# One row of decays a head for pairs 1 to 5 of a decay-attention kernel, the other blocks' masked rows written by GpSimd, and the order of instructions set anew

## The chip, the cores and the metric

The kernel runs on one core of one Trainium2 chip. A core has five engines, each with its own queue of instructions worked off in order: PE (TensorE, matmuls and transposes into PSUM), DVE (VectorE), ACT (ScalarE), POOL (GpSimd) and SP (SyncE, which here only issues DMAs). They meet at semaphores alone. The metric is the device time of one execution in microseconds (us); less is better. Line numbers L... are those of the kernel before, unless said otherwise.

## The reference

Causal attention with a decay for 8 batches of 8 heads, 576 positions, 64 columns a head, and behind it a gated layer with a convolution of 5 taps. Cut to what matters:

```
scores = q @ k.T / sqrt(64)
cum    = cumsum(log(clip(f, 1e-4, 1)))
scores = where(causal, -1e9, scores + cum[:, None] - cum[None, :])
attn   = softmax(scores)                       # per row
x      = attn @ v                              # heads side by side: (8, 576, 512)
gate   = sigmoid(causal_conv5(x, conv_w))
out    = (gate * (x @ w_val)) @ w_out          # float32
```

A constant that is the same in a whole row of scores falls out of the softmax. So a row of the decay needs only -cum of the columns and any reference that is common to the row.

## The kernel before

The work goes by pairs of heads, 32 pairs (4 a batch). The 576 rows of a head's scores are cut in four blocks of 128 rows and a last piece of 64; block j needs its first 128(j+1) columns, so the blocks of a head have 128, 256, 384 and 512 columns (EXT), at columns 0, 128, 384 and 768 of a row of 1280 (BOFF). The last pieces of the two heads of a pair share one tile of 576 columns.

For a pair the steps are these. `load_pair` and `load_rest` load q, k, v and the decays. `plan_t` transposes q and k on PE (L524, L531) and evicts them (Xf for pairs 0 to 3; Xh and Xl, a value and its remainder, from pair 4 on). `plan_s` makes the scores on PE in three groups: blocks 3 and 1 of both heads, blocks 2 and 0, the last pieces. For each block DVE adds the decays to the scores and takes the row's extreme in one instruction (L598, "the reduction"), ACT takes the exponential (L602) into P, and any of POOL, DVE and ACT normalizes P (L376 and L374). `plan_pt` transposes P on PE (L643) and evicts it (L369), `plan_pv` multiplies with v (PV), evicts to x, splits x into xh and xl (L712) and does the convolution's taps (L724 and L376). `plan_moe` runs behind every fourth pair: Mv (x times w_val), h (L769), its split into hh and hl (L782), Mo (h times w_out), and the store. The weights w_val and w_out are loaded and split during the first pairs by DVE, ACT and POOL (L822 to L862).

The decays: a table `decd` of 64 rows, one a head, is written to DRAM at the start. A row has the 1280 columns of the four blocks, each with the block's own reference, and 576 for the last piece. From pair 1 on a head's row is spread over 128 partitions by one DMA into the tile `dm` (640 KB, three buffers dm0 to dm2, taken in turn by heads); a second load fills `dl`. Then POOL masks the diagonal squares of the four blocks in place with two `affine_select` instructions (L428), and adds a triangle to `dl` (L431). Pair 0 has its decays put in by PE, and its `dm1` is a memset to zero (L457) with the same mask.

```python
load("dec", 1.6, p + 0.05 * h, dm[m], decd[2 * i + h:2 * i + h + 1, 0:SW].to_broadcast([P, SW]), dk, [("dm", m)])
pool("sel", 0.8, p + 0.2 + 0.05 * h, sel, [("dm", m)], [("dm", m)])
dkey = [("dm", a)] if u < 2 else [("dl", r, 0), ("dl", r, 1)]
```

What sets the order: the steps are entered into a `Plan` with their durations, priorities and the engines that may do them. `Plan.order` lists them engine by engine on a modelled clock. Tables set it: OFF shifts a step's priority by its class and phase of the program, PEN adds to a step's start time on an engine that it may also run on, STICK favours PE instructions of the mode just run. Each engine then runs its list in order, and a wait holds all that is listed behind it on that engine. Where a step may go to several engines the plan also chooses the engine. DMAs stand in SP's list (some early ones in ACT's).

Of the kernel before, what the change touches and what calls it, by code (L numbers as in the profile page):

```python
# [42 lines left out]
OFF = {  # L43
# [11 lines left out]
    "load": (12.4, 68.46, 92.08, 57.68, 91.65, 143.0), "norm": (-52.85, -16.37, 2.57, -148.6, -15.27, -20.52),  # L55
    "rec": (0.68, 86.96, -11.16, -5.51, -2.16, -38.89), "red": (-0.44, -76.99, -63.6, -16.05, -44.87, 4.92),
    "sel": (37.59, 20.57, -11.72, 7.64, 56.84, 101.1), "sig": (0.0, 0.0, 127.6, 262.5, 85.39, 148.2),
    "st0": (-100.8, 0.0, 0.0, 0.0, 0.0, 0.0), "start": (1.05, 0.0, 0.0, 0.0, 0.0, 0.0),
    "tabD": (-71.18, 0.0, 0.0, 0.0, 0.0, 0.0), "warm": (-150.4, 0.0, 0.0, 0.0, 0.0, 0.0),
# [3 lines left out]
}  # L63
PEN = {
# [4 lines left out]
    ("X", "DVE"): (10.66, 6.42, 35.96, 35.67, 3.07, 32.37), ("conv", "ACT"): (37.06, 9.53, 0.39, 7.85, 12.52, 8.12),  # L69
    ("conv", "DVE"): (0.01, 0.0, 0.02, 0.0, 0.09, 1.39), ("conv", "POOL"): (51.47, 31.7, 58.49, 34.72, 29.95, 35.69),  # L70
    ("hh", "ACT"): (0.0, 0.0, 0.0, 0.0, 0.5, 3.04), ("hh", "DVE"): (0.0, 0.0, 1.73, 16.52, 3.91, 0.39),
    ("hl", "DVE"): (0.0, 0.0, 0.45, 0.87, 4.98, 0.0), ("hl", "POOL"): (0.0, 0.0, 0.0, 0.67, 0.0, 30.02),
    ("load", "ACT"): (1.58, 0.0, 0.0, 0.0, 0.0, 0.0), ("norm", "ACT"): (0.44, 0.25, 1.01, 0.21, 1.1, 2.13),
    ("norm", "DVE"): (6.2, 19.99, 21.87, 2.29, 2.56, 0.18), ("norm", "POOL"): (0.63, 17.37, 0.04, 25.85, 0.46, 2.15),
    ("sel", "DVE"): (36.1, 36.18, 41.87, 17.73, 90.83, 1.24), ("sel", "POOL"): (0.65, 0.76, 0.61, 0.6, 1.44, 6.22),
    ("start", "ACT"): (10.22, 0.0, 0.0, 0.0, 0.0, 0.0), ("start", "DVE"): (4.31, 0.0, 0.0, 0.0, 0.0, 0.0),
    ("start", "POOL"): (5.56, 0.0, 0.0, 0.0, 0.0, 0.0), ("wo", "ACT"): (0.0, 0.0, 5.81, 0.0, 0.0, 0.0),
# [4 lines left out]
}  # L82
# [191 lines left out]
def tile_decay_attention_gated_mlp(  # L274
# [134 lines left out]
    def load_rest(i):  # L409
# [12 lines left out]
        for h in range(2 if i else 1):  # L422
            m = (2 * i + h) % NH if i else 1

            def sel(m=m):
                for lo, n, c in ((0, 256, 0), (256, 512, 384)):
                    t = dm[m][:, lo:lo + 2 * n].rearrange("p (b c) -> p b c", b=2)[:, :, c:c + P]
                    nc.gpsimd.affine_select(out=t, in_=t, pattern=[[0, 2], [-1, P]], base=0, channel_multiplier=1,  # L428
                                            compare_op=ALU.is_ge, fill=-BIG)
            pool("sel", 0.8, p + 0.2 + 0.05 * h, sel, [("dm", m)], [("dm", m)])  # L430
        any_("sel", {"POOL": 0.3, "DVE": 0.14}, p + 0.3, lambda eng: eng.tensor_tensor(  # L431
# [18 lines left out]
    def mk_pick():  # L450
        nc.gpsimd.memset(pick, 0.0)
        for row, cols in ((0, slice(0, P + D)), (D + 1, slice(0, P)), (D + 1, slice(P + D, 2 * P))):
            n = cols.stop - cols.start
            nc.gpsimd.affine_select(out=pick[:, cols], in_=pick[:, cols], pattern=[[0, n]], base=-row, channel_multiplier=1,
                                    compare_op=ALU.not_equal, fill=1.0)
    pool("start", 1.5, z + 0.25, mk_pick, (), [("dm", 0)])
    any_("start", {"POOL": 1.4, "DVE": 0.75}, z + 0.25, lambda eng: eng.memset(dm[1], 0.0), (), [("dm", 1)])  # L457
    any_("start", {"POOL": 0.65, "DVE": 0.4}, z + 0.25, lambda eng: eng.memset(dl[0], 0.0), (), [("dl", 0, 0), ("dl", 0, 1)])
# [459 lines left out]
```

## Time and profile before

| | |
|---|---|
| time, median of 3 runs | 593.08 us (592.48 to 595.91) |
| the profiled execution's own time | 592.27 us |
| its span, first to last instruction | 590.5 us |
| mean granted PE clock | 0.977 |
| loads of `dm`, 640 KB each | 62, 5.4 us from issue to landing (median) |
| POOL selects on `dm` | 126, 481 ns (mean) |

The profile is of one execution. Busy time of an engine leaves out waits and the issuing of DMAs. PEclk is the share of its full clock that PE was granted, in tenths. "Idle before" in a row is the time that the engine stood ahead of these instructions, with what ended it. In a timeline the first two columns are the start and the length of a group in us, and a bracket gives the wait ahead of it.

### The profile page before, as it was taken

Reading aid. Unit: us, or ns where it says so; the run is one execution under the profiler, and the core shown is the slowest. Engines: PE = TensorE matmul, PEld = TensorE weight load, DVE = VectorE, ACT = ScalarE, POOL = GpSimd, SP = SyncE. Lnnn points to the kernel's source line nnn. Section 1 sums busy time; section 2 is a strip of 40 time slices with the busy share of each in tenths; the row PEclk is TensorE's granted clock in tenths of the full one; section 3 lists DMA queues with packets and bytes.
Section 4 is the critical chain, followed back from the end, with each engine's and each line's share of the span. In section 5 each row is a group of like instructions: output and inputs, shape, how many; then the busy total and the mean of one; then the engine's idle time right before and its main releaser. Section 6 shows DMA issues by size and latency. Waiting matters only on the chain.

```text
span 590.5 us, 14025 instructions
## 1 busy us (share of the span) xinstructions
PE 558.2 (95%) x4693; PEld 487.5 (83%) x4693; DVE 461.3 (78%) x1238; ACT 447.9 (76%) x1217; POOL 249.9 (42%) x398
## 2 busy tenths in 40 slices
PE   8778898799889999999999999999999999999997
PEld 7546587689779998889989988899888987889885
DVE  6488979899988797788967897668879789587660
ACT  4688878999878887888887988677798876764511
POOL 3431367334322556456553746455556461210200
PEclk9779699899999999999999999999999999999999
DMA  6979898676465585757866675466776544220012
GB/s 147 266 185 266 170 240 230 166 196 168 114 183 135 143 234 158 188 136 188 188 157 167 184 189 154 117 179 152 193 201 188 159 120 123 80 83 19 37 37 89
DMA packets 136294, 93.43 MB, mean 158 GB/s; under 512 B 118474, under 2 KB 118494, under 8 KB 136222
## 3 DMA queue, kind: packets, MB, share of 16 engines
q1 hardware_dynamic: 136142, 92.52, 59.0%
q8 instruction: 37, 0.61, 0.4%
q14 instruction: 35, 0.29, 0.2%
q10 hardware_dynamic: 80, 0.02, 0.0%
HBM read 82.60 MB, written 9.91 MB: 157 GB/s over the span
## 4 chain that ended last, share of the span: by engine, by line
PE 69%; DVE 13%; DMA 8%; ACT 5%; issue 3%; SPq 1%; POOL 1%; DVEq 0%; POOLq 0%; ACTq 0%
PE banks L354 54%; PE banks L643 9%; DVE banks L598 6%; PE banks L524 3%; DMA wu<-in_moe_w_val_dram 3%; ACT P L602 3%; DMA dm<-decd 2%; DVE gate L724 2%; PE banks L661 2%; DMA qn<-in_q_dram 1%; DVE negm L598 1%; SPq L381 1%; DMA kn<-in_k_dram 1%; PE banks L531 1%; ACT P L374 1%
## 5 line engine op out<-in xcount | busy, mean ns | idle before, releaser
L602 ACT ACTIVATE P<-banks,negm 128x256 f32<-128x256 f32 (+3 forms) x256 | 131.9, 531 | 35.9 <-DVE negm L598 35.6
L369 ACT COPY pt<-banks 128x256 f32<-128x256 f32 (+2 forms) x320 | 116.9, 436 | 42.8 <-PE banks L643 36.4
L598 DVE CUSTOM_DVE_ANT_0 banks<-banks,dm 128x256 f32<-128x256 f32 (+3 forms) x256 | 120.4, 515 | 33.4 <-PE banks L354 22.2
L724 DVE SCALAR_TENSOR_TENSOR gate<-x,cw,gate 128x576 f32<-128x576 f32 x128 | 111.6, 876 | 1.7
L354 PE MATMUL banks<-xh,wall 128*128 128x288 f32 x512 | 110.2, 300 | 1.0 <-ACT ot L369 0.7
L428 POOL TENSOR_SCALAR_AFFINE_SELECT dm<-dm 128x256 f32<-128x256 f32 x126 | 57.5, 481 | 122.0 <-DMA dm<-decd 100.1
L376 POOL TENSOR_SCALAR P<-P,rz 128x128 f32<-128x128 f32 (+3 forms) x132 | 79.0, 614 | 56.5 <-DVE rz L612 32.7
L643 PE MATMUL banks<-ident,P 128*128 128x128 f32 x640 | 93.2, 283 | 9.3 <-POOL P L376 4.1
L354 PE MATMUL banks<-pt,vt 128*64 128x128 f32 (+2 forms) x1408 | 99.0, 294 | 3.2 <-DVE Xl L515 1.9
L354 PEld LDWEIGHTS banks<-pt,vt 128*64 128x64 f32 x1408 | 87.1, 139 | 16.0 <-issue 3.1
L354 PE MATMUL banks<-wall,hh 128*128 128x512 f32 x288 | 92.8, 403 | 2.8 <-ACT P L602 2.6
L643 PEld LDWEIGHTS banks<-ident,P 128*128 128x128 f32 x640 | 74.4, 144 | 20.0 <-POOL P L376 5.3
L354 PEld LDWEIGHTS banks<-xh,wall 128*128 128x128 f32 x512 | 83.8, 188 | 2.8 <-ACT ot L369 1.1
L354 PE MATMUL banks<-xl,wall 128*128 128x288 f32 x256 | 75.4, 294 | 0.0
L712 POOL TENSOR_TENSOR xl<-x,xh 128x576 fp32r<-128x576 f32 x32 | 47.1, 1475 | 46.1 <-ACT xh L369 46.1
L354 PEld LDWEIGHTS banks<-wall,hh 128*128 128x128 f32 x288 | 51.0, 188 | 13.3 <-ACT P L602 3.6
L354 PE MATMUL banks<-Xh 128*128 128x288 f32 (+2 forms) x280 | 59.1, 346 | 1.2 <-DVE Xl L515 1.0
L782 POOL TENSOR_TENSOR hl<-h,hh 128x576 fp32r<-128x576 f32 (+2 forms) x36 | 36.9, 1032 | 48.4 <-ACT hh L369 48.4
L354 PE MATMUL banks<-wall,hl 128*128 128x512 f32 x144 | 56.5, 392 | 0.0
L354 PE MATMUL banks<-Xh,Xl 128*128 128x288 f32 (+2 forms) x280 | 53.6, 315 | 0.0
L354 PE MATMUL banks<-Xl,Xh 128*128 128x288 f32 (+2 forms) x280 | 53.3, 314 | 0.0
L602 ACT ACTIVATION_READ_ACCUMULATOR P<-banks,negm 128x1 f32 x256 | 52.9, 206 | 0.0
(105 smaller groups left out, 916.7 us busy)
## 6 DMA issues: line engine op xcount, KB each, us to landing
dm<-decd SPq DMA_DIRECT2D x62, 640.0 KB, 5.4
out_dram<-ot SPq DMA_DIRECT2D x36, 256.0 KB, 2.1
dl<-decd SPq DMA_DIRECT2D x62, 144.0 KB, 3.8
qn<-in_q_dram SPq DMA_DIRECT2D x64, 128.0 KB, 3.6
kn<-in_k_dram SPq DMA_DIRECT2D x64, 128.0 KB, 5.8
vt<-in_v_dram SPq DMA_DIRECT2D x64, 128.0 KB, 2.9
zn<-in_k_dram SPq DMA_DIRECT2D x32, 32.0 KB, 3.1
vt<-in_v_dram SPq DMA_DIRECT2D x32, 32.0 KB, 3.2
```

Of the source, the lines that this page charges most:

```text
L354: nc.tensor.matmul(out, lhsT=lhsT, rhs=rhs, start=start, stop=stop)
L369: (eng.copy if eng is nc.scalar else eng.tensor_copy)(out=out, in_=in_)
L376: eng.tensor_scalar(out=out, in0=in_, scalar1=col, scalar2=0.0, op0=ALU.mult, op1=ALU.add)
L428: nc.gpsimd.affine_select(out=t, in_=t, pattern=[[0, 2], [-1, P]], base=0, channel_multiplier=1, compare_op=ALU.is_ge, fill=-BIG)
L524: nc.tensor.transpose(out=bank(key)[:, n * P:(n + 1) * P], in_=src[:, n].rearrange("p h d -> p (h d)"), identity=ident)
L598: nc.vector.tensor_tensor_reduce(out=sl, in0=sl, in1=add[:, o:o + ext], op0=ALU.add, op1=ALU.min, scale=-0.125, scalar=3.0e38, accum_out=n ...
L602: nc.scalar.activation(out=dst[:, o:o + ext], in_=bank(key)[:, c0:c0 + ext], func=AF.Exp, bias=negm[r][:, col], scale=-1.0, accum_out=zs[r ...
L643: nc.tensor.transpose(out=bank(key)[:, c:c + P], in_=Pt[m][:, BOFF[b] + P * j:BOFF[b] + P * j + P], identity=ident)
L661: nc.tensor.transpose(out=bank(key)[:, P * j:P * j + P], in_=Pl[r][:, D + P * j:D + P * j + P], identity=ident)
L712: any_("xl", {"POOL": 1.4, "DVE": 0.67}, p, lambda eng: eng.tensor_tensor(out=xl[s], in0=xv, in1=xh[s][:, :].bitcast(F32), op=ALU.subtract ...
L724: eng.scalar_tensor_tensor(out=gt, in0=src, scalar=wt_, in1=gt, op0=ALU.mult, op1=ALU.add)
L782: eng.tensor_tensor(out=hl[jj][:, y:y + x1 - x0], in0=h32[:, x0:x1], in1=hh[jj][:, y:y + x1 - x0].bitcast(F32), op=ALU.subtract)
```

## The change

For pairs 1 to 5 (i < NE = 6) the load of a head's decays brings the row of block 3 alone, 512 columns in place of 1280 (256 KB in place of 640). POOL then writes the masked rows of the blocks 1, 2 and 0 from the first 256, 384 and 128 columns of that row, one `affine_select` each that masks as it copies, and masks the last 128 columns of block 3 in place. The rows of the blocks 0 to 2 thus have block 3's reference. The work stands in two steps of two instructions: blocks 1 and 3, which the first group of reductions needs, and blocks 2 and 0 with a key of their own (`dmb`), which the second group waits for. From pair 6 on everything is as before. The tables OFF and PEN and STICK have other numbers, so every engine's list is another.

```diff
+NE = 6
-STICK = 18.18
+STICK = 20.75
 OFF = {
-    "H": (0.0, 0.0, 6.66, 25.1, 5.83, 28.91), "Mo": (0.0, 0.0, 0.53, 3.6, 3.84, 5.39),
+    "H": (0.0, 0.0, -20.85, -33.12, -47.53, -65.58), "Mo": (0.0, 0.0, -16.69, 18.48, 3.88, 41.67),
...
-            load("dec", 1.6, p + 0.05 * h, dm[m], decd[2 * i + h:2 * i + h + 1, 0:SW].to_broadcast([P, SW]), dk, [("dm", m)])
+            lo = BOFF[3] if i < NE else 0
+            load("dec", 1.6 * (SW - lo) / SW, p + 0.05 * h, dm[m][:, lo:], decd[2 * i + h:2 * i + h + 1, lo:SW].to_broadcast([P, SW - lo]), dk,
+                 [("dm", m), ("dmb", m)])
...
-            pool("sel", 0.8, p + 0.2 + 0.05 * h, sel, [("dm", m)], [("dm", m)])
+
+            def spread(blocks, m=m):
+                for j in blocks:
+                    t = dm[m][:, BOFF[3]:BOFF[3] + EXT[j]]
+                    if j == 3:
+                        t = t[:, L0 - P:]
+                        nc.gpsimd.affine_select(out=t, in_=t, pattern=[[-1, P]], base=0, channel_multiplier=1,
+                                                compare_op=ALU.is_ge, fill=-BIG)
+                    else:
+                        nc.gpsimd.affine_select(out=dm[m][:, BOFF[j]:BOFF[j] + EXT[j]], in_=t, pattern=[[-1, EXT[j]]], base=P * j,
+                                                channel_multiplier=1, compare_op=ALU.is_ge, fill=-BIG)
+            if 0 < i < NE:
+                pool("sel", 0.75, p + 0.2 + 0.05 * h, lambda spread=spread: spread((1, 3)), [("dm", m)], [("dm", m)])
+                pool("sel", 0.9, p + 0.25 + 0.05 * h, lambda spread=spread: spread((2, 0)), [("dm", m)], [("dmb", m)])
+                continue
+            pool("sel", 0.8, p + 0.2 + 0.05 * h, sel, [("dm", m)], [("dm", m), ("dmb", m)])
...
-                dkey = [("dm", a)] if u < 2 else [("dl", r, 0), ("dl", r, 1)]
+                dkey = [("dm", a), ("dmb", a)][:1 + u] if u < 2 else [("dl", r, 0), ("dl", r, 1)]
```

In all, 10 of the 62 loads of `dm` are of 512 columns; POOL has 106 of the old selects, not 126, and 40 new ones (10 of 256, 10 of 384 and 20 of 128 columns). The counts of steps that moved from one engine to another are small: eight more first taps of the convolution on ACT and eight fewer on DVE, four more full `hh` casts on DVE and four fewer on ACT, the memset of `dm1` on POOL and not on DVE.

SP's list ahead of and behind the load of `dm2`, the decays of pair 1's first head (vt1 is pair 1's v, dl1 its last pieces' decays, ot the first piece of w_val). Before:

```order
L381 DMA kn1_76<-in_k_dram 128x4x64 x2
L381 DMA zn1_78<-in_k_dram 64x2x64
L381 DMA vt1_92<-in_v_dram 128x4x64
L381 DMA dm2_70<-decd_67 128x1280
L381 DMA dl1_72<-decd_67 64x576 x2
L381 DMA vt1_92<-in_v_dram 128x4x64
L381 DMA vt1_92<-in_v_dram 64x2x64
L381 DMA ot_125<-in_moe_w_val_dram 128x1024
L381 DMA dm0_68<-decd_67 128x1280
L381 DMA dm1_69<-decd_67 128x1280
```

And now:

```order
L385 DMA kn1_76<-in_k_dram 128x4x64 x2
L385 DMA zn1_78<-in_k_dram 64x2x64
L385 DMA vt1_92<-in_v_dram 128x4x64 x2
L385 DMA dm2_70<-decd_67 128x512
L385 DMA dl1_72<-decd_67 64x576 x2
L385 DMA vt1_92<-in_v_dram 64x2x64
L385 DMA ot_125<-in_moe_w_val_dram 128x1024
L385 DMA dm0_68<-decd_67 128x512
L385 DMA dm1_69<-decd_67 128x512
```

Both halves of pair 1's v stand ahead of the load of `dm2`, not one; the three loads of decays are the shorter ones.

POOL's list at the same place. P0 and P1 are pair 0's P, Pl0 its last pieces, rz0 its row sums' reciprocals; dm2 and dm0 are pair 1's decays, dm1 the first head's of pair 2. Before:

```order
L376 TENSOR_SCALAR P0_83<-P0_83,rz0_97 128x512
L428 AFFINE_SELECT dm2_70<-dm2_70 128x2x128 x2
L376 TENSOR_SCALAR P0_83<-P0_83,rz0_97 128x256
L376 TENSOR_SCALAR P1_84<-P1_84,rz0_97 128x256
L376 TENSOR_SCALAR P0_83<-P0_83,rz0_97 128x128
L376 TENSOR_SCALAR P1_84<-P1_84,rz0_97 128x384
L376 TENSOR_SCALAR P1_84<-P1_84,rz0_97 128x128
L376 TENSOR_SCALAR Pl0_86<-Pl0_86,rz0_97 128x576
L428 AFFINE_SELECT dm0_68<-dm0_68 128x2x128 x2
L428 AFFINE_SELECT dm1_69<-dm1_69 128x2x128 x2
```

And now (L442 masks block 3, L445 writes another block):

```order
L380 TENSOR_SCALAR P0_83<-P0_83,rz0_97 128x512
L445 AFFINE_SELECT dm2_70<-dm2_70 128x256
L442 AFFINE_SELECT dm2_70<-dm2_70 128x128
L445 AFFINE_SELECT dm2_70<-dm2_70 128x384
L445 AFFINE_SELECT dm2_70<-dm2_70 128x128
L380 TENSOR_SCALAR P1_84<-P1_84,rz0_97 128x256
L380 TENSOR_SCALAR P0_83<-P0_83,rz0_97 128x128
L380 TENSOR_SCALAR P1_84<-P1_84,rz0_97 128x128
L380 TENSOR_SCALAR Pl0_86<-Pl0_86,rz0_97 128x576
L445 AFFINE_SELECT dm0_68<-dm0_68 128x256
L442 AFFINE_SELECT dm0_68<-dm0_68 128x128
L445 AFFINE_SELECT dm1_69<-dm1_69 128x256
```

Two of pair 0's normalizations left POOL (ACT has them), and the selects on `dm2` are four. Further on the second two selects of a head may stand behind the first two of the next head: for `dm0` here, and likewise for `dm2` of pair 2, whose rows are now:

```order
L883 TENSOR_TENSOR wall_126<-gate1_114,ot_125 128x512
L445 AFFINE_SELECT dm2_70<-dm2_70 128x256
L442 AFFINE_SELECT dm2_70<-dm2_70 128x128
L445 AFFINE_SELECT dm0_68<-dm0_68 128x256
L442 AFFINE_SELECT dm0_68<-dm0_68 128x128
L445 AFFINE_SELECT dm2_70<-dm2_70 128x384
L445 AFFINE_SELECT dm2_70<-dm2_70 128x128
L445 AFFINE_SELECT dm0_68<-dm0_68 128x384
```

Here `dm0` is the first head of pair 3, and the blocks 2 and 0 of `dm2` come behind its first select.

DVE's list in pair 7, where the first batch's gated layer begins (h32 is the product with the gate, dm0 and dm2 pair 7's decays). Before:

```order
L769 TENSOR_TENSOR h32_116<-banks_129,gate0_113 128x288
L828 TENSOR_SCALAR wu_127<-wu_127 128x512
L724 SCALAR_TENSOR_TENSOR gate1_114<-x321_100,cw_66,gate1_114 128x576
L611 TENSOR_SCALAR rz1_98<-zs1_96 128x5
L612 RECIPROCAL rz1_98<-rz1_98 128x5
L769 TENSOR_TENSOR h32_116<-banks_129,gate0_113 128x288
L832 SCALAR_TENSOR_TENSOR gate1_114<-wu_127 128x512
```

And now:

```order
L790 TENSOR_TENSOR h32_116<-banks_129,gate0_113 128x288
L380 TENSOR_SCALAR gate1_114<-x321_100,cw_66 128x576
L745 SCALAR_TENSOR_TENSOR gate1_114<-x321_100,cw_66,gate1_114 128x576
L790 TENSOR_TENSOR h32_116<-banks_129,gate0_113 128x288
L373 CAST hh0_117<-h32_116 128x576
L803 TENSOR_TENSOR hl0_121<-h32_116,hh0_117 128x576
L619 ISA banks_129,negm1_94<-banks_129,dm2_70 128x384
```

Both parts of the split of h, the cast to hh and the subtraction for hl, stand on DVE for this batch, where ACT and POOL had them; pieces of the weights' work (L828, L832) stand further ahead.

More of the change, by code (lines that the diff above doesn't have):

```diff
@@ L43 @@
 OFF = {
[11 rows of a table removed]
[L55 to L59, printed above, removed]
[3 rows of a table removed]
[11 rows of a table added]
@@ new lines @@
+    "load": (75.64, 91.56, 134.3, 40.19, 88.06, 166.1), "norm": (-57.15, 19.09, 28.6, -105.0, -13.72, 60.39),
+    "rec": (1.94, 79.52, -2.6, 9.19, -23.95, -40.17), "red": (-25.05, -128.4, -70.43, -32.19, -72.71, 2.34),
+    "sel": (54.52, 44.0, -46.39, -77.37, 24.87, 107.0), "sig": (0.0, 0.0, 91.99, 261.8, 91.84, 158.4),
+    "st0": (-113.6, 0.0, 0.0, 0.0, 0.0, 0.0), "start": (-22.35, 0.0, 0.0, 0.0, 0.0, 0.0),
+    "tabD": (-23.73, 0.0, 0.0, 0.0, 0.0, 0.0), "warm": (-190.4, 0.0, 0.0, 0.0, 0.0, 0.0),
[3 rows of a table added]
@@ L63 @@
 }
 PEN = {
[4 rows of a table removed]
[L69 to L77, printed above, removed]
[4 rows of a table removed]
[5 rows of a table added]
+    ("conv", "ACT"): (4.72, 0.0, 4.77, 0.01, 4.04, 1.15), ("conv", "DVE"): (0.11, 0.0, 0.21, 0.04, 0.02, 1.84),
@@ new lines @@
+    ("conv", "POOL"): (47.78, 26.36, 64.53, 25.55, 36.5, 62.0), ("cut0", "ACT"): (0.01, 0.0, 0.0, 0.0, 0.0, 0.0),
+    ("cut0", "DVE"): (0.03, 0.0, 0.0, 0.0, 0.0, 0.0), ("hh", "ACT"): (0.0, 0.0, 1.03, 0.0, 0.0, 1.92),
+    ("hh", "DVE"): (0.0, 0.0, 0.11, 1.8, 11.03, 0.0), ("hl", "DVE"): (0.0, 0.0, 0.0, 0.0, 0.83, 0.0),
+    ("hl", "POOL"): (0.0, 0.0, 6.22, 1.64, 0.36, 6.35), ("load", "ACT"): (2.45, 0.0, 0.0, 0.0, 0.0, 0.0),
+    ("load", "SP"): (0.07, 0.0, 0.0, 0.0, 0.0, 0.0), ("norm", "ACT"): (0.08, 0.22, 0.0, 0.47, 1.37, 19.11),
@@ L82 @@
+    ("norm", "DVE"): (20.64, 27.42, 32.53, 1.55, 17.97, 0.23), ("norm", "POOL"): (0.39, 14.17, 0.0, 30.9, 0.04, 2.48),
+    ("sel", "DVE"): (57.76, 65.08, 75.61, 43.93, 111.3, 34.11), ("sel", "POOL"): (1.27, 0.89, 0.03, 1.13, 0.08, 3.57),
+    ("start", "ACT"): (44.25, 0.0, 0.0, 0.0, 0.0, 0.0), ("start", "DVE"): (11.75, 0.0, 0.0, 0.0, 0.0, 0.0),
+    ("start", "POOL"): (1.2, 0.0, 0.0, 0.0, 0.0, 0.0), ("wo", "ACT"): (0.0, 0.0, 1.11, 0.0, 0.0, 0.0),
[5 rows of a table added]
 }
@@ L455, in mk_pick @@
                                     compare_op=ALU.not_equal, fill=1.0)
-    pool("start", 1.5, z + 0.25, mk_pick, (), [("dm", 0)])
-    any_("start", {"POOL": 1.4, "DVE": 0.75}, z + 0.25, lambda eng: eng.memset(dm[1], 0.0), (), [("dm", 1)])
+    pool("start", 1.5, z + 0.25, mk_pick, (), [("dm", 0), ("dmb", 0)])
+    any_("start", {"POOL": 1.4, "DVE": 0.75}, z + 0.25, lambda eng: eng.memset(dm[1], 0.0), (), [("dm", 1), ("dmb", 1)])
     any_("start", {"POOL": 0.65, "DVE": 0.4}, z + 0.25, lambda eng: eng.memset(dl[0], 0.0), (), [("dl", 0, 0), ("dl", 0, 1)])
```

44 rows, old and new, of tables (OFF, PEN) are left out of this document.

## The prediction

> **What bounds the kernel now.** I read the page first, then the windows by stage, then the waits of each engine, then the timeline of the first pairs. The page gives the busy time of each engine, and PE's busy share, granted clock and DMA share in 40 slices:
>
> ```profile
> span 590.5 us, 14025 instructions
> PE 558.2 (95%) x4693; PEld 487.5 (83%) x4693; DVE 461.3 (78%) x1238; ACT 447.9 (76%) x1217; POOL 249.9 (42%) x398
> PE   8778898799889999999999999999999999999997
> PEclk9779699899999999999999999999999999999999
> DMA  6979898676465585757866675466776544220012
> ```
>
> PE is full from about the thirteenth slice on. What it loses, it loses before that, where its clock also falls. The windows (columns: length, then busy time and instructions of PE, PEld, DVE, ACT, POOL, then PE clock, DMA share, GB/s) are cut at the first reduction (L598) of pair 0, 1, 4, 7, 9 and 10:
>
> ```profile
> 0.00:11.40 11.40, 9.30 (x50) 7.89 (x52) 6.62 (x19) 4.69 (x9) 4.10 (x24) 1.00 0.64 140
> 11.40:31.70 20.30, 16.19 (x121) 12.34 (x119) 11.24 (x33) 12.57 (x35) 9.32 (x18) 0.83 0.91 234
> 31.70:80.20 48.50, 39.66 (x262) 29.04 (x260) 40.25 (x113) 40.83 (x114) 15.95 (x27) 0.82 0.87 218
> 80.20:123.80 43.60, 38.15 (x359) 32.59 (x355) 41.57 (x113) 39.80 (x110) 21.27 (x37) 0.96 0.77 197
> 123.80:155.50 31.70, 30.35 (x288) 27.26 (x285) 29.26 (x84) 29.71 (x83) 13.80 (x18) 1.00 0.69 189
> 155.50:183.00 27.50, 24.64 (x183) 21.02 (x181) 23.20 (x52) 21.89 (x51) 6.38 (x9) 1.00 0.49 133
> 183.00:540.00 357.00, 354.05 (x3157) 317.71 (x3155) 284.29 (x776) 281.54 (x781) 175.59 (x269) 1.00 0.58 156
> ```
>
> Length less busy times clock is what PE lost in a stretch, in time at full clock: 6.9 us from 11.4 to 31.7 (20.30 - 16.19 x 0.83), 16.0 from 31.7 to 80.2, 7.0 to 123.8, 1.4 to 155.5, 2.9 to 183, and 3.0 in the 357 us after that. PE's instructions are the same in both kernels, so the change is worth what it takes from these losses, some 34 us from 11.4 to 183. There DVE and ACT are busy too: from 80.2 to 123.8 DVE is at 95% (41.57 of 43.60) and ACT at 91%. DMA is at 0.91 and 0.87 in the first two of these stretches, but a busy queue is not a wait. The waits of DVE and PE from 31.7 to 183 and, last, two of 0 to 130 (waiter, releaser, us in total, times, longest):
>
> ```profile
> DVE gate L376 <- ACT x L369: 5.2, 2, 3.6
> DVE banks L598 <- PE banks L354: 5.0, 5, 2.0
> DVE gate L824 <- DMA wu<-in_moe_w_val_dram: 1.3, 1, 1.3
> PE banks L531 <- DMA zn<-in_k_dram: 0.9, 1, 0.9
> ...
> POOL dm L428 <- DMA dm<-decd: 22.0, 10, 5.5
> ACT gate L822 <- DMA wu<-in_moe_w_val_dram: 1.9, 2, 1.5
> ```
>
> So the loads of decays make POOL wait for 22 us, but DVE and PE, once pair 1 has begun, hardly wait for a DMA: 1.3 and 0.9 us. Who waits for POOL's selects, up to 140 us, is told by the tile dm:
>
> ```profile
> who waited for it (us, times):
>   POOL dm L428: 28.6, 12
>   DVE banks L598: 1.0, 1
>   PEld banks L643: 0.3, 1
> ```
>
> The 1.0 us is pair 0's, whose dm is not loaded. From pair 2 on the shorter load therefore mostly shortens a wait that nobody inherits. Pair 1 is the exception, since there the select stands ahead of other work on POOL:
>
> ```profile
> 14.99 0.45 SPq L381 DMA_DIRECT2D dm<-decd  x1
> 21.01 0.77 POOL L428 TENSOR_SCALAR_AFFINE_SELECT dm<-dm 128x256 f32<-128x256 f32 x2 [4.41 <-DMA dm<-decd]
> 21.76 2.20 POOL L376 TENSOR_SCALAR P<-P,rz 128x256 f32<-128x256 f32 x5
> 22.29 2.85 PE L643 MATMUL banks<-ident,P 128*128 128x128 f32 x12 [3.45 <-POOL P L376]
> 26.22 3.50 PE L354 MATMUL banks<-pt,vt 128*64 128x128 f32 x44
> 29.66 2.43 PE L354 MATMUL banks<-gate 64*128 64x512 f32 x16
> 31.72 0.69 DVE L598 CUSTOM_DVE_ANT_0 banks<-banks,dm 128x512 f32<-128x512 f32 x1
> ```
>
> POOL sits 4.41 us in front of that select with pair 0's normalizations behind it, PE waits 3.45 us for these, and transposes, pair 0's PV and pair 1's scores follow in PE's order up to the reduction at 31.72.
>
> **The change, part by part.** Prices, mean ns before the second bar or min/median/max, come from these rows (the windows 0 to 130 for POOL, 31.7 to 183 or the whole span for DVE):
>
> ```profile
> L428 POOL TENSOR_SCALAR_AFFINE_SELECT dm<-dm 128x256 f32<-128x256 f32 x32 | 14.1, 465 | 36.2 <-DMA dm<-decd 22.0 <-DVE dm L457 6.1 <-DVE rz L612 6.0
> L454 POOL TENSOR_SCALAR_AFFINE_SELECT dm<-dm 128x192 f32<-128x192 f32 x1 | 0.3, 348 | 0.1
> L454 POOL TENSOR_SCALAR_AFFINE_SELECT dm<-dm 128x128 f32<-128x128 f32 x1 | 0.3, 294 | 0.1
> L376 POOL TENSOR_SCALAR P<-P,rz 128x128 f32<-128x128 f32 x8 | 3.3, 416 | 0.0
> L376 POOL TENSOR_SCALAR P<-P,rz 128x256 f32<-128x256 f32 x7 | 3.3, 481 | 0.0
> L724 DVE SCALAR_TENSOR_TENSOR gate<-x,cw,gate x128: 778/816/1989, 36.7 to 562.3; 128x576 f32<-128x576 f32 x128
> L782 DVE TENSOR_TENSOR hl<-h,hh 128x576 fp32r<-128x576 f32 x4 | 3.0, 758 | 0.3
> L369 DVE CAST hh<-h 128x576 fp32r<-128x576 f32 x4 | 1.8, 453 | 0.0
> L598 DVE CUSTOM_DVE_ANT_0 banks<-banks,dm 128x512 f32<-128x512 f32 x19 | 12.8, 710 | 3.7 <-PE banks L354 3.7
> L457 DVE MEMSET dm<- 128x1280 f32 x1 | 1.1, 1125 | 0.2 <-issue 0.2
> ```
>
> *Start.* The memset of dm for pair 0 (1.13 us) goes from DVE to POOL, which had been idle; in its place DVE takes three evictions of transposes that ACT did. DVE's reduction of pair 0 no longer waits 1.0 us for the select, but its scores may come a little later, as DVE evicts after its table cuts. I take -0.3 us, between -1.0 (the whole wait) and +0.5 (about half the time of the memset that DVE no longer does, spent on evictions).
>
> *Shorter load, pair 1.* A load has 128 x 768 floats less, 393 KB. From 11.4 to 31.7 the queue moved 234 GB/s at a share of 0.91, 257 GB/s at a full share, so 1.5 us less. One half of v of pair 1 (131 KB, 0.5 us) now goes ahead of the load: -1.0 us. The select grows from two instructions (0.77 us) to four: two of 128 columns (2 x 0.294), one of 256 (0.409 undisturbed, half of the timeline's pair being 0.39) and one of 384, on the slope of the two L454 rows (54 ns for 64 columns) 0.51: together 1.5 us, +0.7. Behind it stand three normalizations, not five, as ACT takes over the others: 0.48 + 2 x 0.42 = 1.3 us for 2.2, -0.9. POOL is done 1.2 us earlier, and I take -1.0 for PE and for pair 1. Ends: 0 (the queue is no faster) and -3.45 (PE's whole wait).
>
> *Shorter loads, pairs 2 to 5, and the bytes that other loads no longer queue behind.* Eight loads, 12 us of queue time less. What can be had is what ends in a DMA: DVE's 1.3, ACT's 1.9 and PE's 0.9 us. I take DVE's alone, -1.3, since the weight piece is decoded on DVE's queue; ends 0 and -4.1. If the cover goes, it is POOL's own idle time that shrinks, which costs nothing.
>
> *More work on POOL.* Ten heads at 0.73 us, 7 us, on an engine that is busy 16 of 48.5 us in one stretch and 21 of 43.6 in the next: it fits, 0 by itself. What it can cost is DVE time. L724, four a pair, has a median of 816 ns, 38 above its minimum, with single ones up to 1989, so some meet POOL. If every one of POOL's further instructions that falls into an L724 held DVE for its whole time, it would be 7 us times the share of time that L724 fills: four of 0.82 us in some 17 us a pair (pair 4 to 10 take 102.8 us), 0.2, so 1.4 us. I take +0.4, ends 0 and +1.4. The Trainium skill (SBUF — State Buffer, "Who interferes with whom") says that a VectorE instruction with at most one SBUF input does not contend with GpSimd, while one with two SBUF inputs blocks against a GpSimd instruction that reads SBUF. The reductions, with one input in PSUM, have a mean of 710 ns with POOL beside them in most cases and the rule agrees; by it only L724 and its like pay; with its full block the sum would be 592.5, without it 591.1, instead of 591.5.
>
> *The order.* DVE has about the same work in all. Counted in the two orders, ahead of pair 9's first reduction DVE has four hh casts, four hl subtractions and five L724 more (1.8 + 3.0 + 4.1 us), some evictions more and some casts and the memset less, about +6 us in all; ahead of pair 10's the sum is level again, and PE's work ahead of pair 9's scores is the same in both. So DVE, 92% busy from 123.8 to 155.5, gets work earlier that it did from 155.5 to 183, where PE lost 2.9 us. ACT has some 7 us more ahead of pair 10. I take +0.6: part of 6 us that must fit into DVE's idle time, most of it given back before 183. Ends -2.9 (PE loses nothing there) and +4.
>
> *Sum.* -0.3 - 1.0 - 1.3 + 0.4 + 0.6 = -1.6 us. The profiled execution took 592.27 us (its span is 590.5), so it becomes 590.7; the median of the runs, 593.08, lies 0.8 above it, and so the forecast is 591.5 us.
>
> **The rivals.** *The queue is the bound early on* (faster by over 1%). For: DMA at 0.91 and 0.87, POOL's 22 us, PE's low clock from 11.4 to 80.2. If DVE, idle 9 of 20.3 us before pair 1, were let off the whole 3.45, the memset's 1.0 and the 4.1 us of DMA waits, 8.5 us go: 584.6. Against: after 31.7 DVE and PE wait for ACT and each other, hardly for loads.
>
> *POOL's order holds the reductions back* (slower). Now the last two selects of one head stand behind the first two of another, so behind that head's load: for pair 2, dm2's blocks 2 and 0 behind dm0's landing. If the reductions of pairs 2 to 5 each stand 2 us for it, at a DVE that is 83% to 95% busy, 8 us come on top: 599.5. Against: those blocks are reduced last in a pair, several us after the first, and the loads are shorter; it decides once a load lands over some 5 us after its neighbour's.
>
> *The order costs what it can* (within 1%): the +4 without the -1.3 gives 596.2. *All is hidden*: pair 1 gains nothing and the sum is 592.5 to 593. *Each further select that meets an L724 holds it*: +1.4 in place of +0.4, 592.5.
>
> **How the numbers follow.** The forecast's case (586.5 to 593) 0.44; the order 0.07, each select holding L724 0.07, all hidden 0.06 (592.5 to 597); queue bound 0.22; POOL's order 0.14. 1%, 5.9 us, is about what a measurement of this kernel can tell from no change. So faster 0.23, same 0.62, slower 0.15. The likeliest case alone spans 586.5 to 593; the range takes in most of the queue's case and half of POOL's: 585 to 598.
>
> **What would show it.** Pair 1's first reduction at about 30.5 us in place of 31.7; POOL's wait for dm well below 22 us with no DVE wait on POOL; DVE's and ACT's busy times within a few us of before; PE's loss from 31.7 to 183 still above 24 us. DVE waiting for POOL dm by more than 2 us would prove me wrong to one side, a loss of PE before 183 under 26 us in all to the other.

## The result and the profile after

The changed kernel is slower: 602.16 us, median of four runs (600.13 to 603.35), where the kernel before took 592.78 us beside it (592.39 to 595.91). The ratio is 1.013, with an interval of 1.0091 to 1.017; taken again later, beside other runs of the kernel before, it is 1.0138 (1.0105 to 1.017). All ratios here compare runs in the chip's fast state and are estimates that are not the quotient of the two medians (1.016 here); one execution of 764.7 us at a granted clock of 0.654, of a list tested below, stays out by this. The forecast was 591.5 us with a range of 585 to 598.

What follows in this section is read from one profiled execution of 600.13 us. Its page, first the rows of busy time and then the 40 slices:

```profile
span 598.4 us, 14095 instructions
...
PE 558.4 (93%) x4693; PEld 485.4 (81%) x4693; DVE 462.6 (77%) x1242; ACT 448.7 (75%) x1211; POOL 266.1 (44%) x420
...
PE   8867797789999999999999999999999999999997
...
PEclk9968999989999999999999999999999999999999
DMA  6888666825665457835666557545766534220012
```

PE, DVE and ACT did the same work within 1.3 us, POOL 16 us more, and DMA's slices are emptier. So none of the three got more to do. The span grew by 7.9 us (598.4 - 590.5), so PE must have been kept from its work, or worked at a lower clock, for that much longer. The windows, with the columns and the cuts of the prediction:

```profile
11.40:31.70 20.30, 17.76 (x142) 12.89 (x138) 13.53 (x46) 14.70 (x44) 8.00 (x19) 1.00 0.87 197
31.70:80.20 48.50, 33.99 (x215) 24.98 (x214) 40.51 (x107) 41.21 (x112) 19.29 (x35) 0.82 0.71 168
80.20:123.80 43.60, 35.69 (x339) 29.93 (x341) 40.77 (x113) 41.34 (x111) 22.42 (x35) 0.92 0.77 200
123.80:155.50 31.70, 29.71 (x264) 27.25 (x258) 30.37 (x76) 27.04 (x78) 7.55 (x10) 1.00 0.43 126
155.50:183.00 27.50, 26.79 (x217) 22.21 (x217) 21.06 (x52) 26.39 (x59) 7.64 (x12) 1.00 0.62 168
183.00:540.00 357.00, 351.79 (x3115) 313.02 (x3112) 284.06 (x785) 276.58 (x775) 190.06 (x284) 1.00 0.56 157
```

Length less busy time times clock, in time at full clock, gives PE's loss in each stretch: 2.5 us from 11.4 to 31.7 (6.9 before), 20.6 to 80.2 (16.0), 10.8 to 123.8 (7.0), 2.0 to 155.5 (1.4), 0.7 to 183 (2.9), and 5.2 to 540 (3.0). The same stretch of time holds other work in the two kernels, so a single row is only a hint, but the picture is plain: 4.4 us are won before pair 1, 6.8 us are lost from 31.7 to 183, and behind 183, where the kernel before lost next to nothing, 2.2 us more go. These rows give 4.6 of the 7.9 us; 0.5 more lies ahead of 11.4 (PE busy 8.77 there, 9.30 before), 0.4 behind 540, and the rest, 2.4 us, may lie in clocks rounded to hundredths and modelled ends of matmuls.

The new rows are not what is waited for. The waits of POOL from 0 to 130 us on the loads of decays, and DVE's longest waits from 31.7 to 183 (waiter, releaser, us in total, times, longest):

```profile
POOL dm L445 <- DMA dm<-decd: 12.7, 7, 4.6
...
POOL dm L434 <- DMA dm<-decd: 3.6, 3, 1.8
```

```profile
DVE banks L619 <- PE banks L358: 6.8, 5, 2.0
DVE banks L619 <- ACT pt L373: 2.0, 1, 2.0
DVE gate L373 <- PE banks L552: 1.8, 1, 1.8
```

POOL waits 16.3 us for these loads, 22.0 before, and among DVE's waits in that stretch none names POOL. What PE waited for from 31.7 to 183 is longer. The longest waits of the changed kernel, and then of the kernel before:

```profile
PE banks L664 <- ACT P L378: 6.6, 3, 2.5
PE banks L358 <- DVE gate L373: 3.3, 1, 3.3
PE banks L358 <- ACT P L623: 2.1, 3, 0.9
PE banks L552 <- DMA zn<-in_k_dram: 2.0, 1, 2.0
PE banks L664 <- POOL P L380: 1.7, 3, 0.7
```

```profile
PE banks L524 <- ACT P L602: 4.0, 3, 2.2
PE banks L354 <- ACT P L602: 3.8, 3, 2.4
PE banks L643 <- ACT P L374: 3.3, 3, 2.9
PE banks L354 <- DVE Xl L515: 2.9, 3, 1.0
```

L378 is ACT's normalization, L374 before: the transposes of P (L664) wait 6.6 us for it, where it was 3.3. In the early pairs the new order moved normalizations from POOL to ACT, and ACT is busy 95% of the stretch from 80.2 to 123.8 (41.34 of 43.60). But this is not the whole. Added up over all rows of the two answers, PE's waits grew from 17.9 to 24.5 us, and by releaser they are:

| PE waited for | before | changed |
|---|---|---|
| ACT's normalization | 3.3 | 6.9 |
| ACT's exponential | 8.1 | 3.1 |
| ACT's evictions | 1.3 | 4.2 |
| DVE | 4.1 | 6.6 |
| POOL | 0.2 | 1.7 |
| DMA | 0.9 | 2.0 |

ACT's three rows together grew by 1.5 us only; the rest is spread over DVE, POOL and a load. At the start the changed kernel does well. Its first pairs, in the timeline:

```profile
15.99 0.45 SPq L385 DMA_DIRECT2D dm<-decd  x1
...
19.89 0.40 POOL L445 TENSOR_SCALAR_AFFINE_SELECT dm<-dm 128x256 f32<-128x256 f32 x1 [2.42 <-DMA dm<-decd]
...
21.25 1.18 POOL L380 TENSOR_SCALAR P<-P,rz 128x256 f32<-128x256 f32 x3
...
21.78 1.31 PE L664 MATMUL banks<-ident,P 128*128 128x128 f32 x10 [1.12 <-POOL P L380]
...
26.78 2.43 PE L358 MATMUL banks<-gate 64*128 64x512 f32 x16
...
28.03 0.70 DVE L619 CUSTOM_DVE_ANT_0 banks<-banks,dm 128x512 f32<-128x512 f32 x1 [0.60 <-POOL dm L445]
```

The load is issued 1.0 us later than before (15.99 for 14.99), and yet the select begins 1.1 us earlier (19.89 for 21.01); POOL's wait fell from 4.41 to 2.42 us, PE's wait for POOL from 3.45 to 1.12 (with 1.22 us just ahead of it for one of the normalizations that ACT now does), and pair 1's first reduction came at 28.03 in place of 31.72. The loss comes behind it.

### The profile page after: what moved, and what is told of

Its sections match the earlier page's. It is cut to its first block, busy times and chain, and to the rows that moved or that the text cites. A ratio compares the mean times of both kernels' runs of the same rounds, so it can differ in the third digit from the quotient of the medians.

```text
span 598.4 us, 14095 instructions
## 1 busy us (share of the span) xinstructions
PE 558.4 (93%) x4693; PEld 485.4 (81%) x4693; DVE 462.6 (77%) x1242; ACT 448.7 (75%) x1211; POOL 266.1 (44%) x420
## 4 chain that ended last, share of the span: by engine, by line
PE 66%; DVE 15%; ACT 10%; DMA 4%; issue 3%; POOL 1%; SPq 0%; DVEq 0%; POOLq 0%; ACTq 0%
PE banks L358 53%; PE banks L664 8%; DVE banks L619 5%; ACT P L623 4%; ACT pt L373 2%; PE banks L682 2%; PE banks L545 2%; DVE gate L745 2%; DVE Xh L373 2%; DMA vt<-in_v_dram 1%; DVE negm L619 1%; ACT P L378 1%; DMA wu<-in_moe_w_val_dram 1%; DMA dm<-decd 1%; PE banks L552 1%
## 5 line engine op out<-in xcount | busy, mean ns | idle before, releaser
L373 ACT COPY pt<-banks 128x256 f32<-128x256 f32 (+2 forms) x320 | 118.1, 440 | 33.5 <-PE banks L664 28.1
L745 DVE SCALAR_TENSOR_TENSOR gate<-x,cw,gate 128x576 f32<-128x576 f32 x128 | 112.2, 880 | 14.1 <-ACT gate L378 12.3
L380 POOL TENSOR_SCALAR P<-P,rz 128x256 f32<-128x256 f32 (+3 forms) x138 | 83.3, 620 | 89.2 <-DVE rz L633 52.7
L664 PE MATMUL banks<-ident,P 128*128 128x128 f32 x640 | 92.1, 280 | 15.3 <-ACT P L378 7.9
L358 PE MATMUL banks<-pt,vt 128*64 128x128 f32 (+2 forms) x1408 | 97.5, 293 | 1.4 <-ACT P L623 0.9
L664 PEld LDWEIGHTS banks<-ident,P 128*128 128x128 f32 x640 | 72.1, 142 | 27.3 <-ACT P L378 8.8
L434 POOL TENSOR_SCALAR_AFFINE_SELECT dm<-dm 128x256 f32<-128x256 f32 x106 | 53.6, 529 | 82.2 <-DMA dm<-decd 72.7
L733 POOL TENSOR_TENSOR xl<-x,xh 128x576 fp32r<-128x576 f32 x32 | 48.7, 1521 | 59.6 <-ACT xh L373 59.5
L358 PEld LDWEIGHTS banks<-xl,wall 128*128 128x128 f32 x256 | 48.1, 188 | 0.2
```

Of the source, the lines that this page charges most:

```text
L358: nc.tensor.matmul(out, lhsT=lhsT, rhs=rhs, start=start, stop=stop)
L373: (eng.copy if eng is nc.scalar else eng.tensor_copy)(out=out, in_=in_)
L380: eng.tensor_scalar(out=out, in0=in_, scalar1=col, scalar2=0.0, op0=ALU.mult, op1=ALU.add)
L664: nc.tensor.transpose(out=bank(key)[:, c:c + P], in_=Pt[m][:, BOFF[b] + P * j:BOFF[b] + P * j + P], identity=ident)
L733: any_("xl", {"POOL": 1.4, "DVE": 0.67}, p, lambda eng: eng.tensor_tensor(out=xl[s], in0=xv, in1=xh[s][:, :].bitcast(F32), op=ALU.subtract ...
L745: eng.scalar_tensor_tensor(out=gt, in0=src, scalar=wt_, in1=gt, op0=ALU.mult, op1=ALU.add)
```

## The experiments

Two theories stood against each other. One: the shorter loads and POOL's further selects did what was forecast, and the new order costs some 10 us. The other: the order is level, and POOL's further work (port, selects in front of other work) costs the time. The ratios are to the kernel before on the same chip, with 95% intervals.

**The loads without the order.** The list of the kernel before is kept to the letter; only what a load brings and what the select's step does is changed.

```diff
-            load("dec", 1.6, p + 0.05 * h, dm[m], decd[2 * i + h:2 * i + h + 1, 0:SW].to_broadcast([P, SW]), dk, [("dm", m)])
+            lo = BOFF[3] if i < 6 else 0
+            load("dec", 1.6, p + 0.05 * h, dm[m][:, lo:], decd[2 * i + h:2 * i + h + 1, lo:SW].to_broadcast([P, SW - lo]), dk, [("dm", m)])
...
-            def sel(m=m):
+            def sel(m=m, i=i):
+                if 0 < i < 6:
+                    for j in (1, 3, 2, 0):
...
```

> Order theory (the new lists cost the time, the short loads and the new selects do not): 588 to 592 us, with pair 1's first reduction earlier than 31.7 us. Rival, selects theory (POOL's further selects and their waits cost the time): 597 to 602 us.

Measured: 0.9946 (0.9922 to 0.9971), 592.72 us for 595.25. It was run again on the chip on which the changed kernel was taken again:

> Order theory: 0.3 to 0.8% faster than before. If the first reading came from the chip: within 0.2% of before.

Measured: 0.9969 (0.9938 to 0.9999), 592.92 us for 594.48, where the changed kernel took 603.09. The loads gain 0.3% to 0.5% by themselves (the two intervals reach from 0.01% to 0.8%), and between the two lists, with the same loads and selects, lie 10.2 us.

**The order without the loads.** The list of the changed kernel is kept; the loads are full, the old two selects stand in the first of the two steps, and the second is empty.

```diff
-            load("dec", 1.6 * (SW - lo) / SW, p + 0.05 * h, dm[m][:, lo:], decd[2 * i + h:2 * i + h + 1, lo:SW].to_broadcast([P, SW - lo]), dk,
+            load("dec", 1.6 * (SW - lo) / SW, p + 0.05 * h, dm[m], decd[2 * i + h:2 * i + h + 1, 0:SW].to_broadcast([P, SW]), dk,
...
-                pool("sel", 0.75, p + 0.2 + 0.05 * h, lambda spread=spread: spread((1, 3)), [("dm", m)], [("dm", m)])
-                pool("sel", 0.9, p + 0.25 + 0.05 * h, lambda spread=spread: spread((2, 0)), [("dm", m)], [("dmb", m)])
+                pool("sel", 0.75, p + 0.2 + 0.05 * h, sel, [("dm", m)], [("dm", m)])
+                pool("sel", 0.9, p + 0.25 + 0.05 * h, lambda: None, [("dm", m)], [("dmb", m)])
```

> Order theory: 600 to 605 us, no faster than the changed kernel, with pair 1's first reduction later than in it. Selects theory: 592 to 596 us.

Measured: 1.0212 (1.0183 to 1.024), 608.02 us for 595.25, more than either theory said. The order alone costs 2.1%, and in it the shorter loads seem to be worth more, 0.8% (1.0212 less 1.013 or 1.0138), some 4.6 us; with these intervals it is 0.8% give or take 0.5%. PE's waits from 31.7 to 183 point to a reason:

```profile
PE banks L664 <- ACT P L378: 6.7, 3, 2.4
PE banks L552 <- DMA zn<-in_k_dram: 6.5, 1, 6.5
```

The first row is the same as in the changed kernel, so it comes with the list. The second was 2.0 there. It is for the last rows of a k, whose load SP issues right behind two loads of decays; with full loads PE goes on 4.1 us later there (at 43.52 us in place of 39.47). That the two loads ahead hold it up is likely, but was not tested by itself.

**POOL's work without the rest.** In the old order with full loads, two further selects a head in pairs 1 to 5, of 256 and 128 columns, mask again what is masked.

```diff
+                if 0 < i < 6:
+                    for j in (1, 0):
+                        t = dm[m][:, BOFF[j]:BOFF[j] + EXT[j]]
+                        nc.gpsimd.affine_select(out=t, in_=t, pattern=[[-1, EXT[j]]], base=P * j, channel_multiplier=1,
+                                                compare_op=ALU.is_ge, fill=-BIG)
```

> If POOL's further work is covered: as before, within 0.3% (591 to 595 us on the scale of before's 593). If it holds DVE or its own queue up: 594 to 598 us.

Measured: 1.0012 (0.9978 to 1.0047), so the work is covered. What it does to DVE is read from the rows of L724 (L729 here) from 31.7 to 130, of the kernel before and of this one, and from this one's reductions from 31.7 to 183:

```profile
L724 DVE SCALAR_TENSOR_TENSOR gate<-x,cw,gate 128x576 f32<-128x576 f32 x23 | 19.0, 825 | 0.2
```

```profile
L729 DVE SCALAR_TENSOR_TENSOR gate<-x,cw,gate 128x576 f32<-128x576 f32 x24 | 20.8, 868 | 0.2
...
L603 DVE CUSTOM_DVE_ANT_0 banks<-banks,dm 128x512 f32<-128x512 f32 x18 | 12.1, 713 | 3.9 <-PE banks L354 3.6 <-POOL dm L428 0.3
```

The mean of L724 rose by 43 ns, 1.0 us over 24 of them; that of the reductions stood (710 before). The second theory falls: it asked for 597 to 602 us with the old list and for 592 to 596 with the new one and full loads, and these runs took 592.72 and 608.02.

**Which pairs' loads.** The old order with pair 1 alone short, and with pairs 1 to 8 short (in the diff above, 2 or 9 for 6).

> If the gain of the short loads is pair 1's alone: as with pairs 1 to 5, 0.4 to 0.6% faster than before (about 590 us). If pairs 2 to 5 carry it by the bytes: within 0.2% of before.

> If bytes matter in pairs 6 to 8 too: 0.7% faster than before or more (587 to 589 us). If the gain ends with the first pairs: as with pairs 1 to 5, or slower by POOL's further selects (590 to 593 us).

Measured: 0.9981 (0.9947 to 1.0015) and 0.9998 (0.9965 to 1.003). Going further than pair 5 showed no gain. How the gain divides between pair 1 and pairs 2 to 5 is not settled: the intervals overlap.

**Sequence or engines.** The plan's list is now given as text, each step with its engine, and `order` follows it; the runs with such a list differ in that text alone, and have the loads and selects of the changed kernel.

```diff
+LIST = (
...
-        for _ in nodes:
+        for item in LIST.split():
+            given = (int(item[:-1]), LETTER[item[-1]])
...
+                    if (n, e) != given:
+                        continue
```

First the new sequence with the engine that the old plan chose for each step, then the old sequence with the new plan's engines. In both, 115 of 3,776 steps change engine, 68 of them normalizations between ACT, POOL and DVE.

> If within the order the choice of engine costs the time (normalizations from POOL to ACT, hh and hl to DVE): 593 to 597 us. If the sequence costs it: 600 to 604 us. Selects theory: 600 us or more.

> If the choice of engine costs the time: 597 to 602 us. If the sequence: 589 to 593 us.

Measured: 1.0245 (1.0223 to 1.0266) and 1.0205 (1.0169 to 1.0241), 610.07 and 607.55 us, more than either half was expected to cost. Neither half carries the cost: each sequence is bad with the other's engines, and the new one is worse with the old engines than with its own. In these four lists a sequence and its engines belong together.

**Where in the program.** The new list up to a pair's first reduction and the old list for the rest, cut at pair 1, 5, 10 and 15; and the converse, the old list first, cut at pair 10 and 15. The theory in these expectations is that the loss lies between pair 5 and 8, and in a trickle behind pair 10.

> If the new order costs its time between pair 5 and pair 8 and behind pair 10: as the old order with short loads, 588 to 592 us. If it costs it by what it does before pair 1: 597 us or more.

> Same theory: the loss up to pair 5 is 1 to 3 us more than in the old order, and nothing behind it: 591 to 596 us. If the order costs it early (work put off or brought forward before pair 5 that is paid for later): 599 us or more.

> Same theory: carries the loss from pair 5 to 8, but not the trickle behind pair 10: 595 to 599 us. If all the loss lies before pair 10: 600 to 604 us.

> If the new order loses between pair 10 and 15: like the changed kernel, 0.7 to 1.2% slower than before. If it loses behind pair 15: as the new order up to pair 10, 0.1 to 0.5% slower.

> Same theory: only the trickle behind pair 10: 593 to 598 us. If that trickle comes from the state that the new start leaves, none of it: 589 to 592 us.

> If the loss behind pair 10 trickles evenly over the later pairs: 0.1 to 0.5% slower than before (594 to 596 us). If it is lost between pair 10 and pair 15: as the old order with short loads, 589 to 592 us.

| list | ratio | interval |
|---|---|---|
| old all through | 0.9946, 0.9969 | 0.9922 to 0.9971, 0.9938 to 0.9999 |
| new to pair 1, then old | 0.9981 | 0.9942 to 1.002 |
| new to pair 5, then old | 0.9999 | 0.9964 to 1.0034 |
| new to pair 10, then old | 1.0028 | 0.9997 to 1.0058 |
| new to pair 15, then old | 1.0114 | 1.0083 to 1.0145 |
| new all through | 1.0130, 1.0138 | 1.0091 to 1.017, 1.0105 to 1.017 |
| old to pair 10, then new | 1.0067 | 1.0033 to 1.0102 |
| old to pair 15, then new | 0.9985 | 0.9958 to 1.0012 |

Each ratio is to the kernel before on its own chip, but the rows come from at least four chips, and a spliced list is a new list at its seam.
From 0.996, the middle of the old list's two, the cost up to pair 10 is 0.7%, in small steps that single intervals do not part; from pair 10 to 15 it is 0.85% more, and behind 15 some 0.2%. Read from the other side: behind pair 10 it is 1.1% (1.0067 less 0.996), behind 15 0.25%, so from 10 to 15 again 0.8%. Both ways give the same piece, 5 us between pairs 10 and 15, where the forecast saw nothing; the intervals leave 2.6 us to either side. The theory does not hold as it was put: from pair 5 to 10 the cost is 0.3%, within the intervals, and behind pair 10 it is no even trickle. The windows there, 183 to 232 us, of the new list to pair 10 and to pair 15:

```profile
183.00:232.00 49.00, 48.81 (x441) 44.14 (x441) 40.06 (x109) 38.35 (x114) 26.84 (x45) 1.00 0.63 165
```

```profile
183.00:232.00 49.00, 46.95 (x434) 41.88 (x434) 39.91 (x109) 39.87 (x116) 21.56 (x35) 1.00 0.52 152
```

With the old list behind pair 10 PE loses 0.2 of 49 us, with the new one 2.0. That is a part of the piece: from 183 to 540 us PE is busy 354.17 of 357 us in the first and 350.50 in the second, 3.7 us less. PE's waits in the second, again from 183 to 232:

```profile
PE banks L833 <- DVE Xl L687: 1.2, 2, 0.9
PE banks L815 <- DVE h L941: 0.3, 1, 0.3
PE banks L815 <- ACT P L774: 0.3, 1, 0.3
PE banks L815 <- POOL P L531: 0.2, 1, 0.2
```

They are short, and on three engines. L833 and L815 are L682 and L664 in the changed kernel, the transposes of P's last pieces and of P, and L687 is L536, the eviction of Xl that frees a bank of PSUM.

**The taps.** One of the new choices stands just ahead of that place: the convolution's first taps of pairs 6 to 10 went from DVE to ACT, and DVE's second tap (L745) waits for them. DVE's waits in the changed kernel from 183 to 232:

```profile
DVE gate L745 <- ACT gate L378: 4.7, 2, 2.5
DVE banks L619 <- DMA dl<-decd: 1.4, 1, 1.4
```

And its window there, in its first profile and in its second:

```profile
183.00:232.00 49.00, 47.56 (x446) 42.97 (x443) 39.52 (x112) 40.54 (x118) 22.54 (x37) 1.00 0.54 154
```

```profile
183.00:232.00 49.00, 46.94 (x427) 41.82 (x425) 41.15 (x110) 40.33 (x117) 22.09 (x36) 1.00 0.52 151
```

So five steps were moved: in the new list the taps back to DVE, directly ahead of the second tap, and in the old list the taps to ACT.

> The changed kernel's list and engines, but the first taps of the convolution of pairs 6 to 10, which its order gave to ACT, stand on DVE again, each directly ahead of the pair's second tap (L745). In the changed kernel DVE waits 4.7 to 6.0 us for ACT's taps from 183 to 232 us, and PE then waits for DVE's Xl. Theory (these taps are what costs 0.85% between pairs 10 and 15): ratio to before about 1.004 to 1.007 in place of 1.0130 and 1.0138, PE busy 48.5 us or more of 49 from 183 to 232 (46.9 and 47.6 in the changed kernel). Rival (DVE would be late at that place anyway, since five taps more are 2.6 us more on its list and its other evictions stand as they stood): 1.011 to 1.015 and PE busy below 48 us there.

> The converse: before's list and engines with the shorter loads, but the first taps of pairs 6 to 10 on ACT, at their old places in the list. Theory (the taps on ACT cost by themselves): 1.002 to 1.006 in place of 0.9946 and 0.9969, with a wait of DVE's L724 line for ACT's gate of 2 us or more behind 120 us. Rival (only the place in the new list makes them late): 0.994 to 0.999.

Measured: 1.0153 (1.0102 to 1.0204) and 0.997 (0.9935 to 1.0006). The theory falls both ways. DVE's waits and the window, both from 183 to 232, in the new list with the taps on DVE:

```profile
DVE gate L536 <- ACT x L529: 2.9, 2, 1.7
DVE banks L775 <- DMA dl<-decd: 1.6, 1, 1.6
```

```profile
183.00:232.00 49.00, 47.73 (x446) 43.27 (x447) 41.07 (x115) 39.12 (x116) 22.92 (x38) 1.00 0.53 155
```

The wait for the tap is gone; DVE waits 2.9 us for ACT's eviction of x instead, ahead of the tap that it now does itself, and PE is busy 47.73 us for 47.56 and 46.94. With the taps on ACT in the old list, DVE waits for them too:

```profile
DVE gate L901 <- ACT gate L534: 3.5, 2, 2.7
```

and there PE is busy 49.00 of 49 us. A wait of DVE of this size cost PE nothing in the one list, and taking it away in the other gave PE between 0.2 and 0.8 of 49 us and the kernel's time nothing.

**The changed code under the old tables.** The plan is made anew with the OFF, PEN and STICK of the kernel before.

> If the new tables are to blame for the order: the plan made with the old tables is within 0.6% of before. If any other order than the old one costs this: 1% slower or more.

Measured: 1.0669 (1.0617 to 1.0721). Its page and two of its waits of PE from 31.7 to 183:

```profile
span 629.7 us, 14049 instructions
...
PE 567.4 (90%) x4693; PEld 492.2 (78%) x4693; DVE 466.8 (74%) x1234; ACT 456.5 (72%) x1231; POOL 253.2 (40%) x408
```

```profile
PE banks L355 <- DVE Xl L533: 9.9, 4, 9.2
PE banks L355 <- ACT gate L370: 4.6, 2, 3.9
```

The split of a step into two for ten heads and a shorter load in the plan's model are enough to make the old numbers give a list that is 40 us worse. The new tables got back most of that, not all.

The changed kernel again, on the chip of the second run of the old order with short loads:

> The changed kernel beside the old order with short loads on the same chip: 1.0 to 1.6% slower than before.

Measured: 1.0138 (1.0105 to 1.017).

## Why the prediction was wrong

**The start** (-0.3, ends -1.0 and +0.5). Wrong in sign. Pair 0's first reduction lies at 12.1 to 12.4 us in the profiles with the new start and at 11.2 to 11.95 in those with the old one: about 0.7 us later, just past the end. That its scores may come later behind DVE's evictions was named; its size was not.

**The shorter loads and POOL's work** (-1.0, -1.3 and +0.4, together -1.9). The sum is right. With the old list it measured -1.8 us (592.92 for 594.48, by the ratio 0.9969) and -3.2 us (0.9946), and POOL's busy time grew by 6.5 and 7.2 us there, the 7 of the forecast. The three parts were not told apart: pair 1 alone gave -1.1 us and POOL's work alone +0.7, each with an interval of 2 us to either side. DVE's wait of 1.3 us for a piece of the weights is gone in both profiles with the old list, as said; in one of them a wait of 1.6 us for a load of decays came in its place. In the changed kernel POOL's own wait for decays fell as said, behind pair 0 and up to 183 us no reduction waited more than 0.6 us for POOL, and L724 paid 1.0 us in the run with POOL's work alone, within 0 and 1.4.

The rule of the Trainium skill that the prediction weighed (SBUF — State Buffer, "Who interferes with whom"; the half on one SBUF input holds there outside the 2-port modes) agrees with these rows: 713 ns for the reductions, whose scores are in PSUM, beside more work on POOL, and 868 ns in place of 825 for L724, which reads SBUF twice. In the changed kernel, whose POOL works at other times, the row from 31.7 to 130 is, and below it that of the run with the new list and full loads:

```profile
L745 DVE SCALAR_TENSOR_TENSOR gate<-x,cw,gate 128x576 f32<-128x576 f32 x21 | 18.9, 905 | 0.3
```

```profile
L745 DVE SCALAR_TENSOR_TENSOR gate<-x,cw,gate 128x576 f32<-128x576 f32 x20 | 19.5, 981 | 0.2
```

The first is 80 ns more a piece, 1.7 us in 21, a little past the end of 1.4. But the second has none of POOL's further selects and is 156 ns above the 825 of before, 3.1 us in 20: what L724 pays depends on what of POOL's work it meets, and so on the list. Sorted by their starts and ends in the traces, those that no POOL instruction overlaps have a mean of 813 ns in the kernel before and 815 in that run, and those that one overlaps 838 and 1091. The forecast priced only the meetings that the further selects add.

Single profiles tell less than the prediction hoped: pair 1's first reduction lay between 29.57 and 31.26 in five runs with short loads and the old list, at 31.72 and 30.35 in two with full loads, and at 28.27 with full loads and the new list. So most of the 3.7 us by which it came earlier is the new list and not the load. The prediction's own signs could not have shown the loss either: the earlier reduction (28.03), POOL's shorter wait (16.3 us) and a PE loss above 24 us up to 183 (34.1) all came, and the last of them had no upper end.

**The order** (+0.6, ends -2.9 and +4). This is the step that failed: it measures 10.2 us with short loads (603.09 for 592.92) and 12.6 us with full ones (1.0212 of 595.25). Three of its parts were wrong.

- Work was counted by engine ahead of a pair, and a surplus of 6 us on DVE and 7 us on ACT was taken as "most of it given back before 183". Such a count tells how much an engine has to do and nothing of how the lists of PE, DVE and ACT interlock. PE lost 6.8 us more from 31.7 to 183, in waits that are spread over all the other engines (17.9 us before, 19.8 and 19.9 in the two profiles of the old list with short loads, 24.5 and 24.7 in the two of the changed kernel), none of which the count shows.
- Behind 183 us the loss of before, 3.0 us in 357, was carried over as a property of the work. It is one of the list: the same work with the new list loses 1.4 to 2.1 us in 49 from 183 to 232 (the changed kernel's two profiles and the list that is new up to pair 15), in waits of 0.2 to 0.9 us.
- The end of +4 was made of DVE's surplus alone. With a list in which PE is busy 95% of the span, the nearest rows for an unknown order would have been PE's losses themselves: 27 us from 31.7 to 183 and, behind it, 357 us with a loss of 3.0, in which a new list can win 3 us at most and lose more.

**The rivals.** The queue as the bound did not come: with short loads and the old list the gain is at most 0.8% by either interval. POOL's order as the one that holds reductions back did not either; that its time, 599.5 us, is the nearest is chance, since from 31.7 to 183 DVE did not wait for POOL. The rival that did come, the order, stood at +4 and 0.07.

**What stays open.** Which of the moved steps between pairs 10 and 15 costs the 5 us. The first taps of the convolution do not. Between the list that is new up to pair 10 and the one up to pair 15, 11 steps change engine: two of these taps, three subtractions for hl (from POOL to DVE), four normalizations from ACT to POOL and one back, and one eviction of x (from ACT to DVE); all else is sequence. None but the taps was tried by itself. The waits are many and short and change their releaser when one step is moved, so it may be no single step; that was not shown. The version that beats both kernels is the plain one, the changed loads and selects in the old list: 0.9946 and 0.9969 against before, and 1.7% less than the changed kernel on the same chip.

## What to carry to other kernels

When a change comes with a new order, cost the two apart and give the order the wider bounds: here the shorter loads with POOL's work were worth -2 to -3 us, where -1.9 had been worked out, and the order +10 to +13. Work counted by engine ahead of a point does not price an order, and a wait of an engine beside PE does not either: taking 4.7 us of DVE's waits for ACT's taps away made the kernel no faster here. Where a plan is searched by tables, fit a small edit into the list that is already good before searching anew, and measure that version first.

## What was not expected of the hardware

In single profiles PE was granted its full clock from 11.4 to 31.7 us (1.00) in the changed kernel, 0.92 in the old list with short loads and 0.83 before, in stretches in which it was busy 17.76, 16.59 and 16.19 of 20.30 us. In the next stretch it was 0.82, 0.89 and 0.82. But the second profile of the changed kernel shows 0.92 in the first of these stretches, so the dip moves between executions of one list too:

```profile
11.40:31.70 20.30, 17.64 (x135) 13.40 (x131) 12.26 (x41) 13.48 (x39) 7.96 (x19) 0.92 0.82 198
```

PE's loss in this stretch is 4.1 us there (20.30 - 17.64 x 0.92) and not 2.5, and so 2.8 us are won before pair 1 and not 4.4.

Over all executions on one chip the mean granted clock was 0.9745 for the changed kernel (6 runs), 0.981 for the old list with short loads (12) and 0.978 for the kernel before (17). The span times what is missing to 1 is 15.3, 11.1 and 13.1 us. So up to 4 of the 10 us between the two lists may come by the granted clock, and so may the whole gain of the short loads on this chip (2.0 us by the clock, 1.8 by the ratio). Whether PE's waits bring the lower clock, or the clock is granted otherwise, no run here shows.
